# A kernel's hand-made scheduler: port reservations for the pairs' sums, and its constants chosen anew

## The chip, the cores and the metric

The kernel runs on one core of one Trainium2 chip. The metric is the time of one execution on the device in microseconds (us); lower is better. Engines: PE is TensorE's matmul and PEld its weight load, DVE is VectorE, ACT is ScalarE, POOL is GpSimd, SP is SyncE, which issues most of the DMAs.

## What is computed

Attention over a window of 128 positions, with a bias that falls with distance, for 4 sequences of 576 positions and 8 heads of 64; its result, 2304 rows of 512, goes through four experts, whose outputs are weighted and summed:

```python
scores = np.where(mask, scale * q @ k.T + bias, -1e9)
attn = exp(scores - max) / (sum + 1e-9)
x = (attn @ v)                        # 2304 x 512
p = domain_probs / (domain_probs.sum(-1, keepdims=True) + 1e-09)
for e in range(4):                    # w1[e]: 512 x 1024, w2[e]: 1024 x 512
    out += p[:, e:e+1] * (np.maximum(x @ w1[e], 0.0) @ w2[e])
```

All is done in float32. For the experts every operand is split into a high part (rounded to the format that TensorE takes in one pass) and a low part (what is left), and a product is three matmuls: high by high, high by low, low by high.

## The kernel before, in words

**Tiling.** The 2304 rows are cut into seven blocks (256, 256, 256 and four of 384). Each expert is cut into four units of 256 hidden columns, 16 units in all. Attention runs by segments, one block by one pair of heads, 28 in all. Scores (line 649) use half of the array's rows, values (line 903) half of its columns, the experts' matmuls the whole array.

**Stages.** Blocks 0 to 2 go through the units in plain matmuls: line 1246 for the very first, line 1338 for x by w1, line 1758 for the result by w2, while attention of the later blocks is woven in. Blocks 3 and 4 are then computed together for 13 of the units by a product scheme with seven products in place of eight (`sevenfold`, line 1395), which needs sums and differences of the weights and of x (`combined`, `differences`; line 1180 adds and subtracts). Blocks 5 and 6 come last, from about 606 us on, in eight pairs of units (`pair`): the two units' hidden results are made by `sevenfold`, and the second product, line 1654, is again done with seven products in place of eight. That needs four sums of the hidden results of both units, S1 to S4, each in two pieces (fi 0 and 1) of 128 by 384, and combinations of both units' w2 (`mixed`). A raw sum lies in a tile w1r (S1, S2) or q (S3, S4). It is split into high (a cast, lines 400 and 401, mostly on ScalarE) and low (a subtraction, line 420, in `minus`); for S1 and S2 the parts go into tiles named xh and xl, and this subtraction is on VectorE alone (gp=False). Results leave PSUM through line 1680 or 1776 (weighted by the probability and added to acc, on VectorE), line 1408 (a copy to SBUF on ScalarE) and others.

**The order.** Nothing is issued in program order. Every operation is entered in a `Plan` with its engine or engines, an estimated time, a due time, and what it reads and writes. `Plan.order` then walks a clock of its own: on each engine it takes, among the operations that are ready at the earliest time (within SLACK), the one with the lowest due; an operation with two possible engines goes to the one that ends it first. The result, sorted by planned start, is the order in which each engine's instructions are issued; the chip then keeps each engine's order and the data's waits, but not the planned times. Buffers are handed out in the same walk. `port` in an operation names the engines on which it takes the port that VectorE and GpSimd share: it then starts no sooner than the port is free, and the port is taken until it ends:

```python
if e in o.port:
    t = max(t, port)
```

After the walk a loop at the end of the kernel gives some GpSimd operations a real wait: those that the plan starts less than CLOSE (1.0 us) after the end of the latest VectorE operation that takes the port.

**The constants.** MARGIN, SECOND and AHEAD place attention's due times; BACK and AGAIN those of the loads that fetch blocks 5 and 6 back; URGENT is how much sooner than TensorE's work its evictions are due; WEARLY how much sooner than their use a unit's weights are due (loads, casts, subtractions); WLATE and AHEAD2 the same for a pair's combined w2 and its sums; HOLDOFF delays the first of these; OPENS moves the first weighting of an output tile; SENT is the planned time of a DMA issue on GpSimd; PATIENCE and FAR let VectorE and GpSimd in the pairs wait for a more pressing operation; STICK is a bonus, in us of due time, with which TensorE stays in half-array work when it is there; SWITCH is the planned cost of a change between half and full array; LATE_T and LATE_V delay attention's transposes and values in the plan. FILL dummy matmuls (line 1825) stand at the end of all due times and fill TensorE's planned gaps.

**Names.** s: scores; t: a row's minimum, sum and reciprocal; pb: attention's weights spread out for the values (line 856, on GpSimd); line 737 adds the guard 1e-9 on ScalarE; w, w2h, w2l: parts of weights; w1r, w2r: loaded weights; line 393 is a load or store on SP's queue, line 1085 a load that GpSimd issues; lines 1424, 1485, 1446 and 1568 are VectorE's steps between the seven products and the hidden results.

Of the kernel before, what the change touches and what calls it, by code (L numbers as in the profile page):

```python
# [17 lines left out]
PE, DVE, ACT, POOL, SP = "PE", "DVE", "ACT", "POOL", "SP"  # L18
# [27 lines left out]
class Plan:  # L46
# [48 lines left out]
    def order(self):  # L95
# [37 lines left out]
        while len(out) < len(self.ops):  # L133
            best = None
            for e, q in queue.items():
# [12 lines left out]
                if least is None:  # L148
# [4 lines left out]
                    (c for c in cands if c[0] <= least + SLACK),  # L153
                    key=lambda c: (c[1].due + (0.0 if c[1].mode == "full" else -STICK if sticks else lone), c[1].n),
                )

                if e in (DVE, POOL) and o.n >= self.strict:
                    soon = [c for c in cands if c[0] <= t + PATIENCE and c[1].due < o.due - FAR and c[0] < t + o.engs[e]]
                    if soon:
# [22 lines left out]
            else:  # L182
                o.end = t + (o.cold if e == PE and t < WARM else o.engs[e])
                if e == PE and t >= WARM:
                    o.end += SWITCH if o.mode != mode else 0.0
                    mode = o.mode
# [20 lines left out]
ISSUE = 0.6  # L207
GUARDED = 1e9
CLOSE = 1.0
AGAIN = 1.498  # L210
DBW = 2.4e5
WARM = 8.0
FILL = 80
PLAIN = 3.7
SWITCH = 0.19
STICK = 49.533
LONE = 0.0
SOON = 1.5
FLIGHT = 9
SLACK = 0.1  # L220
PATIENCE = 0.645
HOLDOFF = -2.753
OPENS = 2.874
FAR = 1.744
EXTRA = 0.03
LATE_S = 0
LATE_T = 0.555
LATE_V = 1.699
TURNS = 8
NSV = 3  # L230
DIRECT = 0
# [8 lines left out]
mm = lambda n: max(0.01 + n * 0.000426, 0.112)  # L240
# [42 lines left out]
def attention_moe(  # L283
# [28 lines left out]
    plan = Plan()  # L312
# [60 lines left out]
    after = sb.tile([P, 2, P], F32, tag="after", name="after")  # L373
# [39 lines left out]
        at_ = (slice(None),) * axis  # L413
        return [[x[(*at_, slice(i * m, i * m + m))] for x in aps] for i in range(2)]

    def minus(o, a, b, n, due, reads, writes, gp=True, after=()):

        def emit(e):
            return [
                by[e].tensor_tensor(out=x, in0=y, in1=f(z), op=ALU.subtract) for x, y, z in pieces(e, n, o(), a(), b())  # L420
            ]

        engs = {DVE: dve(n), POOL: pooled(n)} if gp else {DVE: dve(n)}
        return plan.op(engs, emit, due, reads, writes, port=(DVE, POOL) if gp else (), after=after)

    a, b = EARLY
# [12 lines left out]
    for us, nbs in passes:  # L441
        for j, u in enumerate(us):
# [3 lines left out]
            if nbs[-1] not in (4, 6) and u % 2 == 0 and u + 1 in us:  # L446
                half_of[l], half_of[l + 1] = 0, 1
                for nb in nbs:
                    if isinstance(nb, tuple):
                        n = sum(BLOCKS[b][1] for b in nb)  # L450
# [9 lines left out]
                    n = BLOCKS[nb][1]  # L460
# [36 lines left out]
            for nb in nbs:  # L497
                n = BLOCKS[nb][1]
# [30 lines left out]
    for nb, (s0, n) in enumerate(BLOCKS):  # L529
        for hp in range(NPAIR):  # L530
            g = Rec()
# [81 lines left out]
    def unit(u):  # L613
        g, pk, d = u.seg, u.pk, u.due
        n = pk + P

        o = P - pk
# [17 lines left out]
        hs = slice(2 * g.hp, 2 * g.hp + 2)  # L635
        late, late_t, late_v = (0.0, 0.0, 0.0) if g.plain else (LATE_S, LATE_T, LATE_V)

# [47 lines left out]
        elif edge or pk < P:  # L685
            bb = Buf("x")
            b2 = lambda: bb[:, : 2 * P].rearrange("p (h n) -> p h n", h=2)
            if edge:
# [8 lines left out]
                    port=(POOL,),  # L697
# [56 lines left out]
        for h in range(2):  # L754
            plan.op({ACT: 0.29 + m * 0.00087}, exponents(h), d + 0.4, [(t, h)], [(s, h), (t, 2 + h)])
        plan.op(
            {DVE: 0.08, ACT: 0.25} if g.plain else {ACT: 0.25},
            guarded,
            d + 0.5,
            [],  # L760
# [26 lines left out]
        i = u.q0 // P  # L787
# [16 lines left out]
        if g.plain:  # L804
            for h in range(2):
                cast(
                    lambda h=h: g.pt[h][:, c0 : c0 + w],
                    lambda h=h: tp()[:, h, :],
                    w,
                    d + 0.9,  # L810
                    [bk2],
                    [(g.pt[h], i)],
                    False,
                )
        else:
            wb = Buf("tu")
            quarters.append(wb)
            if through:

                tr = Buf("tr")  # L820
                turned_ = lambda: wb.place
                plan.op(
                    {DVE: dve(2 * P) + 0.02},
                    lambda e: nc.vector.transpose(
                        turned_().rearrange("p (b h c) -> p h b c", b=4, h=2), sv().rearrange("p h (b c) -> p h b c", b=4)
                    ),
                    d + 0.75,
                    both,
                    [(wb, b_) for b_ in range(4)],
                    port=(),  # L830
                )
                load(lambda: tr[:], turned_, 131072, d + 0.8, [(wb, b_) for b_ in range(4)], [tr])
                for b_ in range(4):
                    load(
                        lambda b_=b_: wb.place[32 * b_ : 32 * b_ + 32, :].rearrange("r (a n) -> r a n", a=4),
                        lambda b_=b_: tr[:, 64 * b_ : 64 * b_ + 64].rearrange("(a r) n -> r a n", a=4),
                        32768,
                        d + 0.85,
                        [tr],
                        [(wb, b_)],  # L840
                    )
            else:
                plan.op(
                    {ACT: act(2 * P)},
                    lambda e: nc.scalar.activation(wb.place, bk2[:, : 2 * P], AF.Copy),
                    d + 0.85,
                    [bk2],
                    [(wb, b_) for b_ in range(4)],
                )
            raws_ = [(wb, b_) for b_ in range(4)]  # L850
            spread = lambda slot: g.pt.place[:, slot]

            def side(own):
                sign = 1 if own else -1
                steps = [[32 * sign, 4], [0, 2], [sign, 32]] if through else [[0, 2], [sign, P]]
                return lambda e: nc.gpsimd.affine_select(  # L856
                    out=spread(2 * i + own),
                    in_=wb.place,
                    pattern=steps,
                    base=0,  # L860
                    channel_multiplier=-sign,
                    compare_op=ALU.is_ge if own else ALU.is_gt,
                    fill=0.0,
                )

            if pk:
                for own in (0, 1):
                    plan.op({POOL: 0.47}, side(own), d + 0.95 + 0.2 * own, raws_, [(g.pt, 2 * i + own)])
            else:
                cast(  # L870
                    lambda: spread(2 * i + 1),
                    lambda: wb.place,
                    2 * P,
                    d + 1.0,
                    raws_,
                    [(g.pt, 2 * i + 1)],
                )
# [35 lines left out]
        if jobs:  # L913
            if g.plain:
                ps_ = [(b_, k_) for j in jobs for k_ in j[4] for b_ in g.pt]
            else:
                ps_ = [(g.pt, x) for x in range(2 * len(g.units)) if x or g.units[0].pk]
            plan.op(
                {PE: sum(PLAIN * mm(j[3]) for j in jobs)},
                values,  # L920
                d + 1.3,
                [key_of(g.v), *ps_],
                [g.av, "values"],
                (),
                sum(8 * mmc(j[3]) for j in jobs),
                late=late_v,
                mode="col",
            )

    def gathered(g):  # L930

        n, d = g.n, g.units[-1].due
        gr, at = divmod(g.s0, GROUP)

        cols = slice(at, at + n)
        if g.nb in ASIDE:
            x = Buf("x")
            cast(lambda: x[:, :n], lambda: g.av[:, :n], n, d + 1.4, [g.av], [x], False)
            load(lambda: aside[g.nb, g.hp][:], lambda: x[:, :n], 512 * n, d + 1.6, [x], [("aside", g.nb, g.hp)])
            return  # L940
        xh, xl = groups.setdefault(gr, (Buf("xh"), Buf("xl")))
        part = (g.nb, g.hp)
        xparts.setdefault((g.nb, g.hp), []).append(part)
        cast(lambda: xh[:, g.hp, cols], lambda: g.av[:, :n], n, d + 1.6, [g.av], [(xh, part)], False)
        minus(
            lambda: xl[:, g.hp, cols],
            lambda: g.av[:, :n],
            lambda: xh[:, g.hp, cols],
            n,
            d + 1.7,  # L950
            [g.av, (xh, part)],
            [(xl, part)],
            False,
        )

    def fetched(nb, hp, due):
# [150 lines left out]
    def mixed(w0, w1, due):  # L1107
# [43 lines left out]
        if opening_:  # L1151
            for o in plan.ops[mine:]:
                if all(d.n < mine for d in o.deps):
                    o.late = HOLDOFF

# [118 lines left out]
    def relu(l, nb, fi, src, bk, n, due):  # L1274
# [11 lines left out]
        else:  # L1286
# [22 lines left out]
            ),  # L1309
            due - URGENT,  # L1310
            [bk, key_of(h)],
# [186 lines left out]
    def pair(l0, l1, due, between):  # L1498
# [145 lines left out]
        def multiply(bk, lhs, rhs, new, to, last, part):  # L1644
# [21 lines left out]
            for i in ts:  # L1666
                for b_, c_ in to:
# [20 lines left out]

                    plan.op({DVE: dve(256) + 0.06}, weighted, clock[0] - URGENT - (-OPENS if new_ else 2), [bkey[bk][part], "prob"], [(ac, c_)])
                    if (last[part] if isinstance(last, tuple) else last) and finished:  # L1690
# [192 lines left out]
    for l, nb, due in [*steps, (None, None, now)]:  # L1883
# [10 lines left out]
        if was is not None and was[0] == lastly and (l, nb) != was and not fetches:  # L1894
            for b in ASIDE:
                for hp in range(NPAIR):
                    j = NPAIR * (b - 5) + hp
                    fetches.append(j)
                    fetched(b, hp, max(opened[3] + BACK * (1 + j), opened["2"] + 4 + AGAIN * (j - NPAIR) if b == 6 else 0.0))
            differences((5, 6), opening_of[5, 6])  # L1900
# [59 lines left out]
                    tc.add_manual_dep(o.made[0].ins, d.made[-1].ins.name, behind, reason="port")  # L1960


MARGIN = 8.948
SECOND = 9.67
AHEAD = 13.295
BACK = 14.479
URGENT = 8.93
WEARLY = 12.384
WLATE = 9.01
SENT = 1.0  # L1970
AHEAD2 = 4.943


# [55 lines left out]
```

## Time and profile before

| what | value |
|---|---|
| median of 3 runs | 860.22 us (859.94 to 860.25) |
| the profiled execution | 859.72 us |
| its span, first to last instruction | 857.9 us |
| busy: TensorE, weight loads | 849.4 us (99%), 750.1 us (87%) |
| busy: VectorE, ScalarE, GpSimd | 674.5 us (79%), 384.3 us (45%), 365.9 us (43%) |
| granted TensorE clock | 1.00 all the way |
| HBM | 111.32 MB read, 44.04 MB written, 181 GB/s over the span |

Busy time counts a matmul from its start to its modelled end, and matmuls overlap, so a full TensorE can still be fed late: the distance between two starts tells more than the busy share. The dummy matmuls count as busy, too.

### The profile page before, as it was taken

The page shows a single profiled execution, that of the slowest core. Times are in us where ns is not written, and L with a number is a line of the kernel's source. Part 1 is how long each engine was busy: PE and PEld are TensorE (multiplying, and loading weights), DVE is VectorE, ACT ScalarE, POOL GpSimd, SP SyncE. Part 2 cuts the span into 40 slices and gives each one's busy share as a digit, 9 for nine tenths or more (in the row PEclk, how much of TensorE's full clock was granted, in tenths as well). Part 3 has the DMA queues.
Part 4 walks back from the last instruction along what each step waited for, and adds up shares of the span by engine and source line. Part 5 has one row for each costly group of instructions (what it writes and reads, how often), then busy time and mean ns, then how long its engine had stood idle before and what let it go on. Part 6 is the DMA issues. An engine that isn't in the chain of part 4 may idle for free.

```text
span 857.9 us, 15239 instructions
## 1 busy us (share of the span) xinstructions
PE 849.4 (99%) x5050; PEld 750.1 (87%) x5050; DVE 674.5 (79%) x1622; ACT 384.3 (45%) x1001; POOL 365.9 (43%) x573
## 2 busy tenths in 40 slices
PE   8999999999999999999999999999999999999999
PEld 6888788777777878889988988989999999999998
DVE  6998887577766678749987878878789789779877
ACT  6754454235333246423543444433445554544551
POOL 3146432221332133337651234115576575567553
PEclk9999999999999999999999999999999999999999
DMA  8878766456654467524876565644745534633602
GB/s 236 247 226 264 241 185 174 139 165 189 177 167 142 152 203 213 159 74 159 309 283 245 190 251 185 243 174 138 251 134 191 171 112 160 217 101 127 219 1 75
DMA packets 92463, 156.37 MB, mean 182 GB/s; under 512 B 42848, under 2 KB 63072, under 8 KB 88672
## 3 DMA queue, kind: packets, MB, share of 16 engines
q1 hardware_dynamic: 86528, 125.84, 45.4%
q0 software_dynamic: 5632, 29.36, 10.7%
q8 instruction: 40, 0.66, 0.3%
q14 instruction: 39, 0.32, 0.1%
q10 hardware_dynamic: 224, 0.20, 0.1%
HBM read 111.32 MB, written 44.04 MB: 181 GB/s over the span
## 4 chain that ended last, share of the span: by engine, by line
PE 92%; DVE 5%; ACT 1%; DMA 1%; SPq 1%; issue 0%
PE b L1758 31%; PE b L1395 23%; PE b L1338 18%; PE b L1654 11%; PE b L903 4%; PE b L649 4%; DVE xl L420 2%; DVE acc L1680 1%; DVE b L1424 1%; DVE w1r L1568 1%; PE b L1246 1%; DMA w1r<-in_w 1%; PE b L1825 1%; SPq L393 1%; ACT xh L1563 0%; ACT s L1408 0%
## 5 line engine op out<-in xcount | busy, mean ns | idle before, releaser
L1758 PE MATMUL b<-w2h,halves 128*128 128x512 f32 x612 | 207.5, 394 | 0.0
L1338 PE MATMUL b<-xh,w 128*128 128x512 f32 (+2 forms) x576 | 153.8, 341 | 0.0
L1758 PEld LDWEIGHTS b<-w2h,halves 128*128 128x128 f32 x612 | 114.9, 188 | 25.7 <-issue 2.9
L1776 DVE SCALAR_TENSOR_TENSOR acc<-b,prob,acc 128x512 f32<-128x512 f32 x136 | 101.5, 746 | 31.2 <-PE b L1758 30.5
L1758 PE MATMUL b<-w2l,halves 128*128 128x512 f32 x306 | 120.0, 392 | 0.0
L1338 PEld LDWEIGHTS b<-xh,w 128*128 128x128 f32 x576 | 102.2, 189 | 14.7 <-issue 1.5
L420 POOL TENSOR_TENSOR w<-w1r,w 128x256 fp32r<-128x256 f32 x80 | 59.7, 769 | 119.5 <-DVE w L420 59.1
L856 POOL TENSOR_SCALAR_AFFINE_SELECT pb<-s 128x256 f32<-128x256 f32 x120 | 52.7, 465 | 123.5 <-DMA s<-tr 47.5
L1338 PE MATMUL b<-xl,w 128*128 128x512 f32 (+2 forms) x288 | 97.6, 339 | 0.0
L1295 ACT ACTIVATE halves<-b 128x256 fp32r<-128x256 f32 (+2 forms) x76 | 36.9, 488 | 95.0 <-PE b L1338 93.3
L742 ACT ACTIVATE s<-s,t 128x128 f32<-128x128 f32 x128 | 50.6, 396 | 58.1 <-DVE t L724 57.1
L1680 DVE SCALAR_TENSOR_TENSOR acc<-b,prob,acc 128x256 f32<-128x256 f32 x156 | 66.6, 473 | 9.4 <-PE b L1654 8.2
L1408 ACT ACTIVATE s<-b 128x384 f32<-128x384 f32 x87 | 42.5, 488 | 66.4 <-PE b L1395 66.0
L1302 DVE SCALAR_TENSOR_TENSOR halves<-b,halves 128x256 fp32r<-128x256 f32 (+2 forms) x76 | 41.8, 552 | 36.7 <-ACT halves L1295 36.3
L1395 PE MATMUL b<-xh,w 128*128 128x384 f32 x232 | 68.8, 337 | 0.0
L1758 PEld LDWEIGHTS b<-w2l,halves 128*128 128x128 f32 x306 | 57.5, 188 | 9.1
L400 ACT ACTIVATE w2h<-w2r 128x512 fp32r<-128x512 f32 x81 | 49.2, 624 | 30.2 <-PE b L1758 28.3
L420 POOL TENSOR_TENSOR w2l<-w2r,w2h 128x256 fp32r<-128x256 f32 x54 | 40.8, 776 | 50.8 <-ACT w2h L400 24.1
L1338 PEld LDWEIGHTS b<-xl,w 128*128 128x128 f32 x288 | 54.4, 189 | 6.1
L420 DVE TENSOR_TENSOR w2l<-w2r,w2h 128x512 fp32r<-128x512 f32 x75 | 52.3, 723 | 1.2 <-ACT w2h L400 0.8
L1654 PE MATMUL b<-w2h,xh 128*128 128x256 f32 x144 | 41.3, 287 | 3.9 <-ACT s L1408 3.9
L1395 PEld LDWEIGHTS b<-xh,w 128*128 128x128 f32 x232 | 42.8, 188 | 0.6
(232 smaller groups left out, 2077.9 us busy)
## 6 DMA issues: line engine op xcount, KB each, us to landing
w2r<-in_w SPq DMA_DIRECT2D x59, 512.0 KB, 4.1
w1r<-in_w SPq DMA_DIRECT2D x43, 512.0 KB, 4.7
w<-parked POOLq DMA_DIRECT2D x16, 1024.0 KB, 5.3
parked<-w SPq DMA_DIRECT2D x13, 1024.0 KB, 4.4
tr<-s SPq DMA_DIRECT2D x64, 128.0 KB, 2.8
s<-tr SPq DMA_DIRECT2D x256, 32.0 KB, 2.8
vs<-parked POOLq DMA_DIRECT2D x8, 768.0 KB, 4.8
pt<-parked POOLq DMA_DIRECT2D x8, 768.0 KB, 4.6
```

The lines of the kernel that those rows point to most:

```text
L400: return nc.scalar.activation(o(), i(), AF.Copy)
L420: by[e].tensor_tensor(out=x, in0=y, in1=f(z), op=ALU.subtract) for x, y, z in pieces(e, n, o(), a(), b())
L742: return lambda e: nc.scalar.activation(sv()[:, h, -m:], sv()[:, h, -m:], AF.Exp, bias=t[:, h : h + 1], scale=-1.0, accum_out=t[:, 2 + h : ...
L856: return lambda e: nc.gpsimd.affine_select(out=spread(2 * i + own), in_=wb.place, pattern=steps, base=0, channel_multiplier=-sign, compare ...
L1302: lambda e: nc.vector.scalar_tensor_tensor(out=lo[:, :n], in0=src(), scalar=0.0, in1=f(h[:, :n]), op0=ALU.max, op1=ALU.subtract,),
L1338: nc.tensor.matmul(bk[:, :n], a[0][:, kt, fs], b[:, kt, cols], start=kt == 0 and i == 0, stop=kt == KT - 1 and i == 2,)
L1395: nc.tensor.matmul(bank[:, :n], x(k), y(k), start=new and k == 0 and i == 0, stop=k == 1 and i == 2, skip_group_check=True,)
L1408: {ACT: act(n)}, lambda e: nc.scalar.activation(pv(p), bank[:, :n], AF.Copy), at[0] - URGENT, [bank], [p]
L1654: nc.tensor.matmul(bank[bk][part]()[:, cs], a()[:, ns], b()[:, fi, :], start=new and i != 1 and fi == 0 and j == 0, stop=fi == 1 and j == ...
L1680: nc.vector.scalar_tensor_tensor(out=ac[:, ds], in0=bank[bk][part]()[:, cs], scalar=prob[:, nt, e_ : e_ + 1], in1=ac[:, ds], op0=ALU.mult, ...
L1758: nc.tensor.matmul(bk[:, cs], a[:, ns], b[1][:, fi, cs], start=half != 1 and fi == 0 and j == 0, stop=half != 0 and fi == 1 and j == 2, sk ...
L1776: nc.vector.scalar_tensor_tensor(out=o, in0=i_, scalar=p, in1=o, op0=ALU.mult, op1=ALU.add)
```

## The change

`minus` gets an argument sbuf. With it, the reservation of the shared port changes for calls with gp=False alone: they took no port, and now take it on VectorE, unless sbuf is False. There are two such calls: attention's output (`gathered`), which passes sbuf=False and stays as it was, and the split of the pairs' sums S1 and S2. Beside that, three estimated times of attention's operations and eighteen constants change; no operation is added, removed or given another engine to run on.

```diff
-AGAIN = 1.498
+AGAIN = 7.954
 PLAIN = 3.7
-SWITCH = 0.19
-STICK = 49.533
+VALUED = 2.95
+SWITCH = 0.09
+STICK = 28.201
-PATIENCE = 0.645
-HOLDOFF = -2.753
-OPENS = 2.874
-FAR = 1.744
+PATIENCE = 0.715
+HOLDOFF = 13.788
+OPENS = 5.557
+FAR = 5.041
-LATE_T = 0.555
-LATE_V = 1.699
+LATE_T = 2.206
+LATE_V = 1.903
...
-    def minus(o, a, b, n, due, reads, writes, gp=True, after=()):
+    def minus(o, a, b, n, due, reads, writes, gp=True, after=(), sbuf=True):
...
-        return plan.op(engs, emit, due, reads, writes, port=(DVE, POOL) if gp else (), after=after)
+        return plan.op(engs, emit, due, reads, writes, port=(DVE, POOL)[: 1 + gp] if sbuf else (), after=after)
...
-            {DVE: 0.08, ACT: 0.25} if g.plain else {ACT: 0.25},
+            {DVE: 0.08, ACT: 0.25} if g.plain else {ACT: 0.12},
             guarded,
...
-                    plan.op({POOL: 0.47}, side(own), d + 0.95 + 0.2 * own, raws_, [(g.pt, 2 * i + own)])
+                    plan.op({POOL: 0.42}, side(own), d + 0.95 + 0.2 * own, raws_, [(g.pt, 2 * i + own)])
...
-                {PE: sum(PLAIN * mm(j[3]) for j in jobs)},
+                {PE: sum(VALUED * mm(j[3]) for j in jobs)},
                 values,
...
             [(xl, part)],
             False,
+            sbuf=False,
         )
...
-MARGIN = 8.948
-SECOND = 9.67
-AHEAD = 13.295
-BACK = 14.479
-URGENT = 8.93
-WEARLY = 12.384
-WLATE = 9.01
-SENT = 1.0
-AHEAD2 = 4.943
+MARGIN = 6.247
+SECOND = -6.874
+AHEAD = 30.577
+BACK = 23.895
+URGENT = 10.214
+WEARLY = 3.303
+WLATE = 2.747
+SENT = 0.6
+AHEAD2 = 4.921
```

## Rows read from the trace of the kernel before

**Rows 1.** The page's first part: busy us, share of the span, instructions.
```profile
PE 849.4 (99%) x5050; PEld 750.1 (87%) x5050; DVE 674.5 (79%) x1622; ACT 384.3 (45%) x1001; POOL 365.9 (43%) x573
```
**Rows 2.** Windows: length, then busy PE, PEld, DVE, ACT, POOL, clock, DMA, GB/s.
```profile
150.00:200.00 50.00, 50.00 (x282) 39.27 (x282) 33.60 (x111) 18.55 (x63) 13.73 (x28) 1.00 0.53 157
650.00:700.00 50.00, 48.57 (x346) 47.58 (x345) 43.86 (x82) 25.11 (x53) 33.57 (x48) 1.00 0.43 143
652.00:660.40 8.40, 7.79 (x61) 7.26 (x59) 8.40 (x17) 3.49 (x7) 5.22 (x10) 1.00 0.68 234
```
**Rows 3.** The chain that ended last: start us, us, what.
```profile
652.09 2.69 DVE xl L420 x2
...
806.53 2.69 DVE xl L420 x2
```
**Rows 4.** Timeline of PE: start us, us, engine, line, operation, tiles, forms [idle before].
```profile
654.36 0.28 PE L1654 MATMUL b<-w2h,xh 128*128 128x256 f32 x1
654.48 0.28 PE L1654 MATMUL b<-w2l,xh 128*128 128x256 f32 x1
654.83 0.39 PE L1654 MATMUL b<-w2h,xl 128*128 128x256 f32 x1
...
659.34 0.33 PE L1395 MATMUL b<-xl,w 128*128 128x384 f32 x1
659.51 0.34 PE L1395 MATMUL b<-xh,w 128*128 128x384 f32 x1
660.50 0.35 PE L1654 MATMUL b<-w2h,xh 128*128 128x256 f32 x1 [0.66 <-ACT s L1408]
```
**Rows 5.** Timeline of DVE in the same stretch.
```profile
652.01 2.77 DVE L420 TENSOR_TENSOR xl<-w1r,xh 128x384 fp32r<-128x384 f32 x2
...
658.48 0.63 DVE L420 TENSOR_TENSOR xl<-w1r,xh 128x384 fp32r<-128x384 f32 x1
...
659.50 0.86 DVE L1680 SCALAR_TENSOR_TENSOR acc<-b,prob,acc 128x256 f32<-128x256 f32 x2
```
**Rows 6.** Timeline of POOL, the same pair.
```profile
652.91 1.44 POOL L420 TENSOR_TENSOR xl<-w2r,xh 128x256 fp32r<-128x256 f32 x2
655.78 1.18 POOL L1180 TENSOR_TENSOR w1r<-q,k 128x192 f32<-128x192 f32 x2 [1.44 <-DVE q L1568]
...
668.69 1.44 POOL L420 TENSOR_TENSOR w2l<-v,w2h 128x256 fp32r<-128x256 f32 x2
```
**Rows 7.** Line 420 on DVE, 606 to 858 us: ns min/median/max, first and last start.
```profile
L420 DVE TENSOR_TENSOR xl<-w1r,xh x32: 546/586/2257, 623.1 to 843.6; 128x384 fp32r<-128x384 f32 x32
```
**Rows 8.** Timeline of PE around one segment's values and the next one's scores.
```profile
156.19 0.39 PE L1758 MATMUL b<-w2l,halves 128*128 128x512 f32 x1
156.42 0.39 PE L1758 MATMUL b<-w2h,halves 128*128 128x512 f32 x1
156.74 1.52 PE L903 MATMUL b<-pb,v 128*64 128x128 f32 x16
158.19 1.36 PE L649 MATMUL b<-k,q 64*128 64x256 f32 x12
```
**Rows 9.** Window of line 1246 alone: length, busy PE and PEld, clock, DMA, GB/s.
```profile
0.00:25.40 25.40, 3.36 (x22) 2.78 (x22) 1.00 0.83 250
```
**Rows 10.** Timeline of PE at the start.
```profile
13.11 0.86 PE L903 MATMUL b<-acc,v 128*64 128x256 f32 x6 [0.56 <-ACT acc L400]
```
**Rows 11.** The chain that ended last, in the last pair.
```profile
838.77 1.65 PE b L1825 x15
```
**Rows 12.** Line 1180 on DVE, 606 to 858 us: columns as in rows 7.
```profile
L1180 DVE TENSOR_TENSOR q<-k,w1r x13: 591/868/1091, 630.2 to 815.9; 128x384 f32<-128x384 f32 x13
```
**Rows 13.** Timeline of DVE in the stage of blocks 3 and 4.
```profile
462.50 0.68 DVE L420 TENSOR_TENSOR w<-w1r,w 128x512 fp32r<-128x512 f32 x1
463.38 0.75 DVE L1776 SCALAR_TENSOR_TENSOR acc<-b,prob,acc 128x512 f32<-128x512 f32 x1 [0.19 <-PE b L1758]
```
**Rows 14.** Timeline of PE, the same stretch.
```profile
464.54 0.33 PE L1395 MATMUL b<-xh,w 128*128 128x384 f32 x1
```

## The prediction

> **What bounds the kernel now.** I read the page's busy shares first: TensorE is busy for 849.4 of 857.9 us [rows 1], so only what idles or crawls on TensorE can be won. The table of windows comes next, to find where it idles. A stretch of the attention stage is full, 50.00 of 50.00 us, with VectorE at 33.60; a stretch of the last stage, where pairs of expert units are computed, has 48.57 and VectorE at 43.86 [rows 2]. The missing time is in the pairs, and there VectorE is the engine with the least room. Third, the chain that ended last: in the pairs it leaves TensorE and goes through two subtractions of line 420, 2.69 us for two, first at 652.09 and last at 806.53, with one such piece every 30.9 us, six in all [rows 3].
>
> The timelines say what happens there. TensorE's matmuls of 256 columns start 0.12 us apart; at 654.48 the next one starts 0.35 us later, and at 659.51, where 0.17 would be usual (659.34 to 659.51), the next starts 0.99 us later [rows 4]. So a pair loses 0.23 + 0.82 = 1.05 us. The first loss waits for the low part of a pair's sum. On VectorE the two subtractions starting at 652.01 last 2.77 us together [rows 5]; GpSimd begins its own subtraction (line 420 too, two pieces, 1.44 us) at 652.91, inside them [rows 6]. Over the stage the 32 subtractions xl<-w1r take 546 ns at best and 586 in the median, but 2257 at worst [rows 7]. So one subtraction per pair takes 1.7 us too long (2.25 against 0.55), and it overlaps GpSimd's.
>
> The second loss is the echo of the first. The product that starts at 660.50 goes on in a PSUM bank whose former content VectorE must first weight and add up (line 1680). Those additions start at 659.50, behind more subtractions such as the one at 658.48, and the two that are needed end at 660.36 [rows 5]. VectorE has no gap on the way there, busy for 8.40 of the 8.40 us from 652.0 to 660.4 [rows 2], so a subtraction shorter by 1.7 us lets them end that much sooner, where 0.82 would do.
>
> **The change, part by part.** *Reserving the port.* Only calls with gp=False are touched. The attention's call keeps no port (sbuf=False); the pairs' sums 1 and 2, fi 0 and 1, are the 32 rows xl<-w1r [rows 7]. In the plan they now start only when the port is free, and hold it. On the chip a GpSimd operation that the plan starts within 1.0 us (CLOSE) after such a subtraction also gets a wait for it. Nothing is added or removed on an engine; the wait's price is GpSimd's. It would begin at about 653.1 (652.01 + 2 × 0.55) instead of 652.91, and behind it are the GpSimd subtraction of sum 2's raw value and its cast on ScalarE, due before TensorE's product at 660.50; GpSimd idles 1.44 us before that piece, at 655.78 [rows 6], so 0.2 us are hidden. Gain: 6 pairs × 1.05 = 6.3 us. Lower bound 0 (the collision only moves, or still happens); upper bound 6.3, since TensorE shows no other wait in a steady pair. I take 6.3, because VectorE's lead of 1.7 us is twice the 0.82 that has to go.
>
> The Trainium skill ("SBUF — State Buffer", Who interferes with whom) says that the one that issues first has the shared pair for its whole instruction and the other blocks fully. The trace disagrees: VectorE's subtraction was running when GpSimd began, and VectorE's took 2.25 us while GpSimd's pieces took their usual 0.72 each; by the rule VectorE would have lost nothing there, the 1.7 us would be no matter of the port, and the sum would be rival A's time.
>
> *Attention's estimates.* Three planned costs change: GpSimd's spreading 0.47 to 0.42, the guard on ScalarE 0.25 to 0.12, the values' factor 3.7 to 2.95 (1.71 to 1.36 us for a segment of 384 rows). The trace has 16 of these matmuls, a whole segment, in 158.19 − 156.74 = 1.45 us [rows 8], nearer to the new figure. The two others are on engines with 13.73 and 18.55 busy us of 50. And where attention runs TensorE does not wait [rows 2]: price 0, covered by the expert matmuls between the segments. If that cover breaks, a wait like the 0.82 above is what one costs.
>
> *STICK and SWITCH.* Going from full matmuls to the values' costs 0.32 − 0.23 = 0.09 us (156.42 to 156.74, where the matmul before was followed after 0.23) [rows 8], which the new SWITCH of 0.09 meets. STICK falls from 49.5 to 28.2, so scores stay behind the values less often. In the 24 later segments, each score group that is torn off costs one or two switches: 0 to 24 × 2 × 0.09 = 4.3 us. I take 0.5, about six torn groups, since the bonus is still more than half of what it was.
>
> *The start.* WEARLY falls by 9.1 and SECOND by 16.5, so the first weights can fall behind more of attention's loads on SP's queue. The expert matmuls that now fill TensorE's gaps before 25.4 us are busy for 3.36 us [rows 9], which bounds the loss. TensorE waits 0.56 us at 13.11 for a copy on ScalarE [rows 10], where the cast of those weights stands too, which bounds the gain. I take 0, between ends of 0.56 and 3.36 us, because attention's matmuls, then earlier, would fill the same gaps.
>
> *The last pair* has a hole of 1.65 us at 838.77, filled with dummy matmuls of line 1825 [rows 11]: gain 0 to 1.65; I take 0, as no edit names what it waits for.
>
> *The other constants* (MARGIN, AHEAD, BACK, AGAIN, URGENT, WLATE, HOLDOFF, PATIENCE, FAR, OPENS, SENT, AHEAD2) move due times on every queue, SP's and GpSimd's among them. WLATE makes the pairs' weight splits due 6.3 us later; a split on GpSimd at 668.69 [rows 6] serves the product one pair after 660.50, at 691.4, with some 20 us to spare. LATE_T acts on nothing, as no later segment goes through TensorE's transpose. I price all at 0, hidden by TensorE's backlog, except the rival below.
>
> Sum: 859.72 (the profiled execution: span 857.9 and 1.8 around it) − 6.3 + 0.5 = 853.9 us. The median of the runs, 860.22, is 0.5 above the profiled one, so I forecast **854.4 us**.
>
> **The rivals.** *A: the reservation does not hold on the chip.* The plan's clock drifts from the chip's, and only GpSimd ever gets a wait; or the slow subtraction has another cause than the port. For it: line 1180's operations reserve the port already, and yet q<-k,w1r has a median of 868 ns against a best of 591 [rows 12]. Against it: VectorE starts the two at 652.01 and GpSimd its own at 652.91 [rows 5, 6]; in that order the second ends less than CLOSE before GpSimd begins, and GpSimd gets the wait. The pairs keep 1.05 us: 859.72 + 0.5 + 0.5 = 860.7 us.
>
> *C: only the first loss goes.* The trace names ScalarE's copy of line 1408 as what ended the wait at 660.50 [rows 4]. If it is really that, its own chain (six products, then the copy) is untouched: 6 × 0.23 = 1.4 us gained, 859.3 us. Against it, by the code the product needs neither the copy nor its bank, and VectorE's second addition ends at 660.36, right before the product starts [rows 5].
>
> *B, slower: the weights come late in the stage of blocks 3 and 4.* Thirteen units split their weights on VectorE and GpSimd. The subtraction of w at 462.50 ends at 463.18, ahead of an accumulation of 0.75 us [rows 13], and the first product on the tile w after it starts at 464.54 [rows 14]: 1.36 us of slack. WEARLY makes that split due 9.1 us later, so accumulations may overtake it. One is hidden; with two 0.14 us are lost per unit, and from the third on it decides: 3 × 0.75 − 1.36 = 0.89 us for each of 13 units, 11.6 us, 854.4 + 11.6 = 866.0 us. For it: VectorE is busy there, and the due is what breaks ties. Against it: the split starts as soon as its buffer is free, and due counts only among what is ready.
>
> **How the numbers follow.** The forecast has 0.62, A 0.12, C 0.09, B 0.17. A measurement tells about 0.2% (1.7 us) of this kernel from no change. The forecast is faster by 0.7%; A and C lie within 0.2%; B is slower: 0.62, 0.21, 0.17. The range goes down by the last pair's 1.65, the start's 0.56 and the 0.5 for the switches, to 851.7, and by 1.2 more for orders that I cannot see, to 850.5; up over C and A with 1.3 for torn score groups, to 862. That leaves out B. The forecast's own range is 850.5 to 858.
>
> **What would show it.** Right: xl<-w1r at most some 700 ns in all steady pairs, the two chain pieces of line 420 gone, matmul starts 0.12 apart where 0.35 and 0.99 stood, TensorE near 50.00 in the window 650 to 700. A: 2257 still the worst. C: the short gap gone and the 0.99 still there, ending with line 1408's copy. B: TensorE idle between 400 and 606 us, released by line 420. The forecast is wrong if the pairs' period stays near 30.9 us, or if new idle time before 606 us eats what the pairs give.

## The result, and the profile after

The changed kernel takes **850.92 us** (median of 4 runs, 850.55 to 851.53) where the kernel before takes 860.08 (median of 4, 859.35 to 860.25): a ratio of **0.9896**, with a 95% interval of 0.9879 to 0.9913. That is 9.2 us, faster, inside the range given, and 3.5 us below the forecast of 854.4. The profiled execution took 850.55 us.

The page of the changed kernel, its first two lines and the shares of the chain that ended last:

```profile
span 848.8 us, 15203 instructions
PE 844.5 (99%) x5050; PEld 748.3 (88%) x5050; DVE 662.7 (78%) x1621; ACT 393.3 (46%) x1019; POOL 346.3 (41%) x550
...
PE 98%; DVE 1%; issue 0%; ACT 0%; ACTq 0%
```

TensorE's work is the same 5050 matmuls; 4.9 us of its busy time are gone beside the idle time, because a held matmul and a dummy both count as busy [rows 1]. The windows of the changed kernel, which answer to those of the pairs in [rows 2] (the second lies one pair's work from 651.60 on):

```profile
650.00:700.00 50.00, 50.00 (x364) 50.00 (x363) 42.56 (x91) 25.39 (x53) 29.67 (x45) 1.00 0.46 153
651.60:660.00 8.40, 8.40 (x70) 8.40 (x69) 7.82 (x18) 3.38 (x7) 6.77 (x12) 1.00 0.66 241
```

TensorE is full, and does 364 matmuls in the 50 us in place of 346. VectorE has 0.58 us free in the shorter window, where it had none. Its subtractions of S1 and S2 are short (line 421 now; ns min/median/max, first and last start), against a worst of 2257 ns in [rows 7]:

```profile
L421 DVE TENSOR_TENSOR xl<-w1r,xh x32: 540/549/953, 622.3 to 835.3; 128x384 fp32r<-128x384 f32 x32
```

VectorE's timeline in the same pair as [rows 5]:

```profile
651.67 1.05 DVE L421 TENSOR_TENSOR xl<-w1r,xh 128x384 fp32r<-128x384 f32 x2
...
656.60 1.02 DVE L421 TENSOR_TENSOR xl<-w1r,xh 128x384 fp32r<-128x384 f32 x2
657.57 1.27 DVE L1682 SCALAR_TENSOR_TENSOR acc<-b,prob,acc 128x256 f32<-128x256 f32 x3
```

And GpSimd's, where the wait that the reservation gives shows as idle time ended by VectorE's xl:

```profile
652.88 1.43 POOL L421 TENSOR_TENSOR xl<-w2r,xh 128x256 fp32r<-128x256 f32 x2 [0.23 <-DVE xl L421]
```

The two subtractions last 1.05 us together in place of 2.77, GpSimd's piece begins 0.16 us after they end instead of inside them, and the weighted additions (line 1682 now) end at 658.84, ahead of the product that starts at 659.13. TensorE's timeline at the two places of [rows 4]:

```profile
654.13 0.28 PE L1656 MATMUL b<-w2h,xh 128*128 128x256 f32 x1
654.25 0.28 PE L1656 MATMUL b<-w2l,xh 128*128 128x256 f32 x1
654.37 0.28 PE L1656 MATMUL b<-w2h,xl 128*128 128x256 f32 x1
...
658.96 0.33 PE L1397 MATMUL b<-xh,w 128*128 128x384 f32 x1
659.13 0.28 PE L1656 MATMUL b<-w2h,xh 128*128 128x256 f32 x1
```

The starts lie 0.12 and 0.17 us apart where 0.35 and 0.99 stood. **Where the time came from** is read from the chain that ended last. In it the run of 42 matmuls with which a pair's first products begin comes back once a pair. The kernel before (a run of 42 is cut there into 30 and the pieces behind it):

```profile
641.52 5.23 PE b L1395 x30
...
672.40 5.23 PE b L1395 x30
...
826.85 7.31 PE b L1395 x42
```

The changed kernel:

```profile
641.28 7.30 PE b L1397 x42
...
670.95 7.30 PE b L1397 x42
...
819.25 7.30 PE b L1397 x42
...
829.74 1.43 PE b L1656 x12
831.17 0.45 PE b L1827 x4
831.62 13.53 PE b L1656 x114
```

Up to the first of these rows the profiles differ by 0.24 us (641.52 − 641.28). That tells nothing: two kernels shown below whose order up to there is that of the kernel before (the one wait and the collider twice) reach this row at 640.38 and 640.74. The six pairs that follow take 185.33 us before and 177.97 after, 7.36 us less, 1.23 a pair. From the last row on, the last pair takes 31.05 us to the span's end before and 29.55 after, 1.50 us less: the hole of 1.65 us with 15 dummies [rows 11] has become one of 0.45 with 4. Together these are 9.1 us, the difference of the spans (857.9 and 848.8). What is left to explain: whether the reservation does all this, what the constants do, and whether it is the port.

### The profile page after: what moved, and what is told of

Same layout as the page of the kernel before. It is cut to its first block, busy times and chain, and to the rows that moved or that the text cites. A ratio compares the mean times of both kernels' runs of the same rounds, so it can differ in the third digit from the quotient of the medians.

```text
span 848.8 us, 15203 instructions
## 1 busy us (share of the span) xinstructions
PE 844.5 (99%) x5050; PEld 748.3 (88%) x5050; DVE 662.7 (78%) x1621; ACT 393.3 (46%) x1019; POOL 346.3 (41%) x550
## 4 chain that ended last, share of the span: by engine, by line
PE 98%; DVE 1%; issue 0%; ACT 0%; ACTq 0%
PE b L1760 32%; PE b L1397 25%; PE b L1340 18%; PE b L1656 13%; PE b L904 4%; PE b L650 4%; PE b L1827 1%; PE b L1248 1%; PE b L801 0%; DVE w1r L1182 0%; DVE xl L421 0%; DVE acc L725 0%; DVE b L1426 0%; DVE w1r L1570 0%; DVE q L1570 0%
## 5 line engine op out<-in xcount | busy, mean ns | idle before, releaser
L1778 DVE SCALAR_TENSOR_TENSOR acc<-b,prob,acc 128x512 f32<-128x512 f32 x136 | 101.5, 746 | 32.3 <-PE b L1760 31.3
L421 POOL TENSOR_TENSOR w<-w1r,w 128x256 fp32r<-128x256 f32 x66 | 50.0, 779 | 73.0 <-DVE w L421 32.8
L421 DVE TENSOR_TENSOR w2l<-w2r,w2h 128x512 fp32r<-128x512 f32 x76 | 54.9, 746 | 1.4 <-ACT w2h L401 1.2
L1426 DVE TENSOR_TENSOR b<-b,s 128x384 f32<-128x384 f32 x58 | 32.6, 562 | 13.4 <-PE b L1397 9.1
```

The lines of the kernel that those rows point to most:

```text
L1778: nc.vector.scalar_tensor_tensor(out=o, in0=i_, scalar=p, in1=o, op0=ALU.mult, op1=ALU.add)
```

## The experiments

Each is compared with the kernel before, run on the same chip. Line numbers shift by a few lines between kernels; names say what is meant.

**The reservation alone**, in the kernel before:

```diff
-    def minus(o, a, b, n, due, reads, writes, gp=True, after=()):
+    def minus(o, a, b, n, due, reads, writes, gp=True, after=(), sbuf=True):
...
-        return plan.op(engs, emit, due, reads, writes, port=(DVE, POOL) if gp else (), after=after)
+        return plan.op(engs, emit, due, reads, writes, port=(DVE, POOL)[: 1 + gp] if sbuf else (), after=after)
...
             False,
+            sbuf=False,
```

> The kernel before with the port reservation of the pairs' sums alone, all constants and estimates as before. Theory P (the port collision in six pairs is the cause, and the reservation takes it away): xl<-w1r never over 1 us in the steady pairs, their period 29.7 us in place of 30.9, time 852 to 853.5 us. Rival K (the constants are what helped): the collision only moves, 858.5 to 861 us. If the reservation also explains the last pair, its hole of 1.65 us goes too and the time is near 851.

Measured: 852.16 us against 859.76, ratio 0.9910 (0.9894 to 0.9927), a gain of 7.6 us. Its subtractions and its chain:

```profile
L420 DVE TENSOR_TENSOR xl<-w1r,xh x32: 540/548/905, 623.8 to 837.0; 128x384 fp32r<-128x384 f32 x32
```

```profile
642.15 7.31 PE b L1396 x42
...
671.82 7.31 PE b L1396 x42
...
832.11 1.66 PE b L1826 x15
```

A pair takes 29.67 us, as in the changed kernel; the hole of the last pair stays, 1.66 us with 15 dummies. So the reservation is worth the six pairs' 7.3 us and nothing in the last pair.

**The constants and estimates alone**, the changed kernel with the old reservation:

```diff
-        return plan.op(engs, emit, due, reads, writes, port=(DVE, POOL)[: 1 + gp] if sbuf else (), after=after)
+        return plan.op(engs, emit, due, reads, writes, port=(DVE, POOL) if gp else (), after=after)
```

> The changed kernel with the reservation taken back, so the constants and attention's estimates alone. Theory P: a collision of 2.25 us stays or comes back in the pairs, period 30.5 or more, time 857 to 860 us. Rival K: 851 us as with the whole change.

Measured: 864.85 us, 1.0057 (1.0042 to 1.0072): the constants without the reservation cost 5.1 us, a time that neither theory expected. The collision is there, the longest of the 32 subtractions lasting 2294 ns, and the chain passes through it:

```profile
644.46 5.24 PE b L1397 x30
...
654.93 2.78 DVE xl L421 x2
...
662.23 0.95 DVE halves L421
663.18 0.80 DVE acc L1682 x2
664.11 1.66 PE b L1656 x12
...
833.66 7.30 PE b L1397 x42
```

The span is 863.1. Split as above, against the kernel before: 2.9 us lost up to 644.46, 3.9 lost in six pairs of 31.53 us, 1.6 won in the last pair. In the pairs the second loss grew from 0.82 to 1.48 us: the matmul at 662.46 is followed at 664.11, 1.65 us on where 0.17 is usual, and a subtraction of halves now stands ahead of the additions that the product needs. The first 2.9 us hold one stall of 1.94 us in the first pair and its echo in the clock (last section). So the parts do not add: −7.6 and +5.1 would make −2.5, and together they give −9.2. I read this so: with VectorE's 1.7 us back, the order that the new constants make has the room that it lacks without. No run shows that by itself.

**One wait, and nothing else of the change.** The kernel before with its order untouched; in the six pairs, GpSimd's subtraction xl<-w2r also waits for VectorE's second subtraction of S1. No reservation, no new constants. ScalarE's copy of line 1408, on which rival C rested, keeps its place:

```diff
...
+        for name, o in parts2:
+            if name == 2 and o.eng == POOL:
+                d = [x for x in sums1 if x.eng == DVE and 0.0 < o.start - x.end < CLOSE]
+                if d:
+                    o.after.append(max(d, key=lambda x: x.end))
...
```

(`parts2` lists the subtractions of the combined w2, `sums1` those of S1; both are filled where they are made.)

> The kernel before with its order untouched, and in six pairs one wait added: GpSimd's subtraction xl<-w2r waits for VectorE's second subtraction of sum 1. Theory P: xl<-w1r at most 700 ns there, both stalls of TensorE go, and with them the slow second start behind each (0.10 and 0.08): 6 x 1.23 = 7.4 us, 852.8 us. Rival C (ScalarE's copy ends the longer stall): only the shorter goes, 6 x 0.33 = 2.0 us, 858.2 us. Rival 'not the port': the 2.25 us stay, 860.2 us.

Measured: 851.71 us, 0.9909 (0.9892 to 0.9925), 8.1 us less. No subtraction of S1 or S2 lasts longer than 941 ns, and in the chain the runs of 42 go from 640.38 to 818.42 in six pairs, 29.67 us each. That is 7.3 us; the other 1.1 us of the spans' difference lie ahead of the first run (640.38 against 641.52), where no edit acts. The chain at the last pair:

```profile
830.35 1.65 PE b L1828 x15
```

Six waits give all that the reservation gives. Both losses of a pair go although only the first has to do with this subtraction directly, so the second was its echo. Rival C is false: in the same pair the product now starts at 658.23, before ScalarE's copy, which starts at 658.43. And since GpSimd can be made to wait for VectorE's subtraction, that subtraction needs no result of GpSimd's. The last pair's hole stays, and VectorE's timeline there says what stands ahead of S1's subtractions:

```profile
828.81 0.98 DVE L420 TENSOR_TENSOR xl<-w2r,xh 128x512 fp32r<-128x512 f32 x1
...
830.89 1.01 DVE L420 TENSOR_TENSOR xl<-w1r,xh 128x384 fp32r<-128x384 f32 x2
```

In the last pair VectorE makes the low part of a weight itself. In the changed kernel that piece is GpSimd's (xl<-w2r at 830.90), and S1's two subtractions come at 829.63.

**The collider twice.** If the port is what holds VectorE, a longer GpSimd operation at that place must hold it longer. The kernel before, with GpSimd's xl<-w2r emitted twice in a row (the second writes the same values again):

```diff
-            minus(lo, raw, hi, 512, d, [*rk, hk], [lk])
+            o = minus(lo, raw, hi, 512, d, [*rk, hk], [lk])
+            if name == 2:
+                once = o.emit
+                o.emit = lambda e: [*once(e), *(once(e) if e == POOL else [])]
```

> The kernel before, in which GpSimd runs its subtraction xl<-w2r (two pieces) twice in a row, so four pieces, 2.9 us. If VectorE loses the port for as long as GpSimd goes on: xl<-w1r's worst goes from 2.25 to about 3.7 us and each of the six pairs is 1.4 us longer, 868.8 us. If a collision costs a fixed price, or the 2.25 us have another cause: the worst stays at 2.25 and the time at 860.2 us, as GpSimd has room.

Measured: 867.63 us, 1.0092 (1.0076 to 1.0107), 7.9 us more. The subtractions of S1 and S2, then the timelines of VectorE and GpSimd in one pair:

```profile
L420 DVE TENSOR_TENSOR xl<-w1r,xh x32: 541/585/3612, 622.4 to 850.9; 128x384 fp32r<-128x384 f32 x32
```

```profile
651.23 4.12 DVE L420 TENSOR_TENSOR xl<-w1r,xh 128x384 fp32r<-128x384 f32 x2
```

```profile
652.14 2.80 POOL L420 TENSOR_TENSOR xl<-w2r,xh 128x256 fp32r<-128x256 f32 x4
```

GpSimd's operation grew by 1.36 us (from 1.44) and VectorE's by 1.35 (from 2.77); a pair takes 32.22 us by the chain's pieces (651.32 to 683.54), 1.33 more than before, and six of them make 8.0. The first loss of a pair grew to 1.58 us and the second is as it was, 0.81: VectorE and TensorE both slip by the same. So the hold has no fixed price: it lasts as long as GpSimd's run.

**The last pair: the weights due later there alone.** The one-wait kernel, with the product 4 of the last pair getting the changed kernel's WLATE:

```diff
-        others = mixed(w0, wst[l1], {k_: x - WLATE for k_, x in ready.items()})
+        others = mixed(w0, wst[l1], {k_: x - (2.747 if ending and k_ == 4 else WLATE) for k_, x in ready.items()})
```

> The kernel of the one wait (e3), and in the last pair alone the split of the weights for the last product (4) due 6.3 us later, as WLATE of the change would have it. Theory W (in the last pair VectorE takes that split, 0.86 + 0.98 us, ahead of sum 1's subtractions, and TensorE stands 1.65 us for them; WLATE moves it behind): the hole with 15 dummies goes, 1.6 us less than e3, near 850.1 us. Rival: the hole only moves to another wait of the last pair, 851.7 us.

Measured: 851.58 us, 0.9912 (0.9897 to 0.9926): no gain over the one wait (851.71). The hole with 15 dummies is gone from its place, and the chain shows the new one:

```profile
832.96 0.96 DVE xl L420
833.92 0.88 DVE q L1181
...
836.22 9.51 PE b L1657 x78
```

TensorE waits for VectorE 6 us further on. Here GpSimd makes that piece of the weight, at 829.85, and it collides with S1's subtractions, which last 1.60 us together (rows in the last section). The rival, that the hole only moves, was right in the time. In the trace, the last product ends 26.5 us after the last run of 42 starts, in place of 27.3 with the one wait alone. But the dummies that no longer stand in the hole now stand at the end of the kernel, 29 in place of 17, and the span ends 4.2 us behind the last product in place of 3.8, so little of it is left.

**WLATE: added to the reservation, and taken out of the change.** Two kernels, one edit each; the first starts from the reservation alone, the second from the changed kernel:

```diff
-WLATE = 9.01
+WLATE = 2.747
```

> The kernel before with the reservation and WLATE = 2.747, nothing else of the change. Theory W: reservation alone (852.2) less the last pair's 1.6 us, near 850.6 us, that is, the whole change's time from two of its edits. Rival (other constants matter too): 852 us or more.

```diff
-WLATE = 2.747
+WLATE = 9.01
```

> The changed kernel with WLATE back at 9.01. Theory W: the last pair's hole of 1.65 us comes back and nothing else, near 852.5 us. Rival (another constant closes the hole): 850.9 us.

Measured: 851.09 us, 0.9904 (0.9890 to 0.9919), and 851.64 us, 0.9912 (0.9896 to 0.9929); both lie between what the theory and its rival gave. In the chain the first has one hole left in its last pair, the second three:

```profile
829.97 0.56 PE b L1826 x5
```

```profile
830.91 0.24 PE b L1827 x2
...
835.46 0.34 PE b L1827 x3
...
838.13 0.34 PE b L1827 x3
```

With the reservation, WLATE closes the hole to 0.56 us, and the other constants without WLATE close it to 0.92 in three pieces. From the start of the last run of 42 to the span's end are 31.3 us with the reservation alone, 30.6 with WLATE beside it, 30.3 with all but WLATE, and 29.6 in the changed kernel. So WLATE and the others give about half of the 1.5 us each; which of the others act was not tried. A part of what WLATE wins is gone again at the end: 31 dummies stand there in place of 17, and the span ends 4.5 us behind the last product in place of 4.1 (3.7 in the changed kernel, with 13 dummies). That the dummies are the cause is not shown. The times of these kernels, of the change, of the reservation alone and of the one wait lie between 0.9896 and 0.9912 with intervals that overlap. Only their traces tell them apart, and none beats the changed kernel clearly.

**The estimates alone**: the kernel before with the guard at 0.12, the spreading at 0.42, the values' factor at 2.95 and SWITCH at 0.09, nothing else:

> The kernel before with attention's three estimated costs and SWITCH as changed (spreading 0.42, guard 0.12, values 2.95, SWITCH 0.09), nothing else. Theory: attention is hidden behind the experts' matmuls, so TensorE's time up to 600 us stays within 0.5 us, and the pairs keep their collision: 859 to 861 us. Rival (truer estimates alone are worth something): under 858 us. If the pairs' order is touched as well, the time can leave both, and the pairs' period tells it.

Measured: 872.58 us, 1.0152 (1.0137 to 1.0168): **13 us slower**, where my sum had 0. The last of attention's values starts at 386.4 us (376.1 in the kernel before), and then TensorE runs out of work; the window of 400 to 425 us, and in TensorE's timeline the matmul after the longest stall:

```profile
400.00:425.00 25.00, 19.86 (x100) 17.19 (x99) 24.04 (x36) 10.46 (x19) 11.51 (x13) 0.89 0.51 176
```

```profile
420.31 2.29 PE L1395 MATMUL b<-kl,w 128*128 128x384 f32 x6 [4.18 <-DVE x L1485]
```

VectorE is busy for 24.04 of the 25 us there: when attention ends late, the sums and differences that open the stage of blocks 3 and 4 fall together, and VectorE becomes the bound. In the kernel before, and in the changed one, TensorE is busy for all 25.00 us of that window.

**AHEAD: added to the estimates, and taken out of the change.** AHEAD says how long before the stage of blocks 3 and 4 the plan wants attention to end. The first kernel is the one just shown with

```diff
-AHEAD = 13.295
+AHEAD = 30.577
```

> The kernel with attention's estimates alone (e9), and AHEAD = 30.577 as changed. Theory H (the shorter estimates let attention end later on the chip against the stage of blocks 3 and 4, which needs all of it, 386 in place of 376 us, and AHEAD is what moves it forward again): the last values start before 378 us, TensorE's 11 us of loss between 400 and 425 us go, and the time is back at 859 to 861.5 us with the pairs' collision as before. Rival (another constant does that, or the loss has another cause): 868 us or more.

and the second is the changed kernel with AHEAD at 13.295 again.

> The changed kernel with AHEAD back at 13.295. Theory H: attention ends some 10 us later, the stage of blocks 3 and 4 begins with a hole on TensorE of 5 to 11 us, 856 to 862 us, and the pairs are as short as with the change (period 29.7 us). Rival (other constants carry attention forward too): 850.5 to 852 us.

Measured: 860.77 us, 1.0007 (0.9998 to 1.0017), and 857.39 us, 0.9969 (0.9957 to 0.9981). The same window of the first, whose last values start at 374.5 us:

```profile
400.00:425.00 25.00, 25.00 (x130) 22.86 (x129) 21.88 (x39) 12.10 (x23) 15.46 (x21) 1.00 0.77 275
```

And of the second, with the last values at 383.3:

```profile
400.00:425.00 25.00, 22.59 (x127) 19.92 (x126) 24.71 (x38) 11.45 (x20) 13.94 (x16) 1.00 0.69 248
```

Attention's end and the window go together in all five kernels: with the last values at 374.4 (the changed kernel), 374.5 and 376.1 (before) the window is full; at 383.3 it lacks 2.4 us of busy time and at 386.4 5.1. So the new estimates alone make attention end too late, and AHEAD takes that back. The pair of them is worth nothing that can be told from noise; the estimates without AHEAD cost 13 us in the kernel before and some 6 in the changed one (0.9969 against 0.9896). AHEAD without the estimates was not run.

## Why the prediction was right, and where its sizes were off

**The port reservation, −6.3.** Right in place and mechanism, short in size. I priced a pair at 0.23 + 0.82 = 1.05 us by the distance of two starts. Each wait also makes the start after it late, and those two starts I had not counted. They stand in TensorE's timeline of the kernel before:

```profile
655.05 0.28 PE L1654 MATMUL b<-w2h,xh 128*128 128x256 f32 x1
...
660.70 0.28 PE L1654 MATMUL b<-w2l,xh 128*128 128x256 f32 x1
```

From 654.83 [rows 4] to 655.05 are 0.22 us, and from 660.50 to 660.70 are 0.20, both 0.12 in a full stretch: 0.18 us more, 1.23 a pair, which is what the periods show. So the term was 7.4 (measured: 7.36), not 6.3, and the 6.3 that I had called its upper bound was none. That the wait's price on GpSimd is hidden held: it idles 0.23 us for it.

**The last pair, 0.** The step that failed: no edit named what the hole waited for, and I took the lower end of 0 to 1.65. It gave 1.5. The order has changed there, by several of the constants together: VectorE no longer splits a weight ahead of S1's subtractions. That is not the whole reason: with the reservation and WLATE it does not either, and that last pair is still 1.0 us longer than the changed kernel's. The rest stays open.

**STICK and SWITCH, +0.5.** It did not show. TensorE's changes between half-array work (scores and values) and the rest, counted over the trace, are 66 before and 68 after; two changes would cost 0.2 us by my 0.09. No run changes the two constants alone, and 0.2 us is less than the stretch up to 641 us varies by.

**Attention's estimates, 0.** The number came out right and its reason did not. I said that matmuls of the experts between the segments cover them. That cover does break, at 400 us: the three new times (with SWITCH, which ran with them) cost 13 us, and AHEAD, which I had put among the other constants at 0, gives all but about 1 of the 13 back. Two large terms cancelled, and that the 0 came out is luck. **The other constants, 0**: luck as well, since without the reservation they and the estimates cost 5.1 us together; with it they give the last pair's 1.5.

**The start, 0.** The wait of 0.56 us at 13.11 [rows 10] is gone, and shorter ones stand elsewhere: over the first 25.4 us TensorE is busy for 23.42 us in place of 23.15. What that is worth cannot be told from how much the stretch up to 641 us varies.

The forecast was 3.5 us too high: 1.1 of it are the pairs, 1.5 the last pair and 0.5 the switches, 3.1 in all.

**Rival A** (the reservation does not hold): false, no subtraction of S1 or S2 is above 953 ns, and that one stands in the last pair. **Rival C** (only the first loss goes): false by the one wait. **Rival B** (weights late in the stage of blocks 3 and 4): did not come; TensorE's losses there are as before. But that stage was where the danger lay: not through WEARLY and the weights, as I had it, but through attention's end.

The prediction also weighed a rule of the Trainium skill ("SBUF — State Buffer", Who interferes with whom), that the one who issues first keeps the shared pair; the page states it for VectorE's two-port modes, and then that the order of issue, not the operation, decides who blocks. In the steady pairs of the kernel before, and with the collider twice, the trace speaks against it: VectorE's record starts 0.39 us ahead of GpSimd's, and VectorE was held to the end of GpSimd's pieces. At other places of these runs the trace agrees with it (last section). So the prediction's "the trace disagrees" is right for the place that it reads, and no more than that.

## What to carry to other kernels

On an engine that has no gap, an operation held by a neighbour costs again wherever that engine's next results are due: price it at each place where the bound engine starts late, and count the late start behind the wait. A scheduler's constants are no independent terms: here new estimates cost 1.5% and a margin gave it back, so a change that moves both must be tested with one of them put back. And where one collision is the cause, a single wait on the engine with slack does what a new plan does.

## What the runs showed of the hardware

**The port.** In the steady pairs of the kernel before, VectorE's subtraction with two inputs in SBUF, whose record starts 0.4 us before GpSimd's, does not finish while GpSimd's pieces run back to back, two or four of them: it ends 0.43 us after the last (652.01 + 2.77 = 654.78 against 652.91 + 1.44 = 654.35) and 0.41 us after it with the collider twice (655.35 against 654.94). GpSimd's pieces keep their pace, 1.44 us for two and 2.80 for four, where two take 1.43 after the wait. The 0.43 us that VectorE still needs are most of the 0.55 that it takes undisturbed, so it had done little by then, and which of the two had the port first the trace cannot tell. An operation of VectorE with one input in PSUM (tile b) is not held: this one of the changed kernel runs inside GpSimd's two pieces (652.88 to 654.31) and takes its usual time:

```profile
653.12 0.54 DVE L1570 SCALAR_TENSOR_TENSOR q<-b,acc 128x384 f32<-128x384 f32 x1
```

It is not always VectorE alone that pays. In the last pair of the one-wait kernel with the weights due later, the same two operations meet with GpSimd's start only 0.13 us behind VectorE's:

```profile
829.72 1.60 DVE L420 TENSOR_TENSOR xl<-w1r,xh 128x384 fp32r<-128x384 f32 x2
```

```profile
829.85 2.07 POOL L420 TENSOR_TENSOR xl<-w2r,xh 128x256 fp32r<-128x256 f32 x2
```

Here VectorE's first takes 0.58 us and its second 1.09, and GpSimd's pieces take 1.06 and 1.05: they end in turn, at 830.30 (VectorE), 830.91, 831.32 and 831.92. In the changed kernel another subtraction of VectorE meets GpSimd once a pair. In four of the six steady pairs GpSimd's piece starts 0.36 to 0.38 us ahead, and VectorE takes 1.23 us and ends 0.55 us behind that piece. In the other two VectorE starts 0.28 and 0.30 us ahead and takes 0.69, and GpSimd's piece is stretched, to 1.01 and 0.98 us, where the next of its kind takes 0.74. With no piece of GpSimd beside it (once, in the last pair) VectorE's takes 676 ns; TensorE does not wait for it:

```profile
L421 DVE TENSOR_TENSOR w2l<-w2r,w2h x7: 676/1225/1227, 660.2 to 812.7; 128x512 fp32r<-128x512 f32 x7
```

So here the one that starts first keeps going. Why the steady pairs of the kernel before go the other way stays open.

**The clock after a stall.** In two runs a stall of TensorE cost a second time. With the constants alone, TensorE idles for 1.94 us before 631.04, in the first pair, and soon after that the granted clock is 0.58 over 3.5 us, between its two levels, 1.2 and 2.4 GHz (windows of that kernel):

```profile
632.50:636.00 3.50, 3.50 (x16) 3.50 (x16) 1.83 (x4) 0.87 (x2) 0.00 (x0) 0.58 0.02 5
```

With the estimates alone, after the 4.18 us idle before 420.31, it is 0.50, the lower level, over six:

```profile
420.00:426.00 6.00, 5.69 (x18) 5.70 (x19) 4.65 (x9) 2.54 (x5) 3.68 (x5) 0.50 1.00 340
```

Matmuls of 384 columns start 0.32 us apart there (422.39, 422.71 and 423.03 in its timeline), where 0.17 is usual. Its chain has 18 of them in 6.11 us where 18 × 0.17 = 3.1 would do, so a stall of 4.2 us cost about 7.
